# A new order of the same instructions: three tables of a planned kernel replaced

## The chip, the cores and the metric

The kernel runs on one core of a Trainium2 chip. The metric is device time in microseconds (us). The kernel before took 600.57 us in the median of 3 runs (599.95 to 601.61).

## The reference

An attention over local windows and block summaries, and then a layer norm with a two-layer network on its result:

```python
k_sum = k.reshape(B, H, nb, 32, D).max(axis=3)          # B, H, S, D = 4, 8, 768, 64
v_sum = v.reshape(B, H, nb, 32, D).mean(axis=3)
scores_l = where(|i - j| < 16, scale * q @ k.T, -1e9)
scores_s = scale * q @ k_sum.T + log(32)
a = softmax(concat([scores_l, scores_s]))
attn = a @ concat([v, v_sum])                            # -> x: (4, 768, 512)
xn = (x - mu) / sqrt(var + 1e-6) * g_ln
out = x + max(xn @ w_ch1, 0) @ w_ch2                     # w_ch1: 512 x 2048
```

## The kernel before, in words

The rows of x are cut into 24 blocks `T` of 128; attention goes in 48 half blocks `t` (four heads each), the network in 12 groups `g` of two blocks. Attention of batch 0 (`early_...`, t below 12) works in float32; the later ones split q, k and v into two float16 parts (`load_q`, `load_k`, `load_v`, `qk`, `softmax`, `transp`, `pv`). The weights are fetched in 32 pieces of 512 KB (`fetch_w`, m = 0 to 31), decoded (`dec_w`, three instructions on VectorE and a sum of squares on ScalarE), scaled by groups (`scale_w`) and converted to two float16 parts (`conv_w`). `g1` and `g2` are the first and second layer of groups 0 to 4; `sp1`, `sp2` and `sw2` do the same for the later groups with fewer products (Strassen-like, with operands made by `combine` and `combine2`). `batch(b)` reads K, q and V of the next batch (`batch_k`, `batch_q`, `batch_v`: a DMA into one of two staging buffers, a reduction on VectorE, absolute values on ScalarE), and `batch_s` makes the scales of the float16 parts.

Nothing is issued as it is written. Each function above is a step; steps are collected first (797 of them) and then recorded in the order of the table `ORDER` (`record_steps`, L230). Recording gives each operation (3501 in all) its dependences and decides who holds a shared buffer or PSUM bank after whom; the bank of each PSUM tile comes from the table `BANKS` (L578). Then `issue` (L538) lays the operations out on the five engines with a list of costs: an engine takes, among what is ready, the operation with the lowest number in the table `RANKS`. The numbers are a permutation of 0 to 3500. All DMAs are issued by SyncE (SP), in its order. In gaps of TensorE that the plan foresees early on, short transposes are put in as filling (`spare`).

A staging buffer is named by `stage_in` (L674): in batch 1 the pieces go in turn into `qs` and `bst` by the parity of a number, so `batch_q(1,5)` and `batch_v(1,3)` share `bst`, and `batch_v(1,2)` and `batch_v(1,4)` share `qs`. The DMA of the next piece waits until ScalarE has taken the absolute values of the one before.

Steps named in the prediction: `batch_k` (L685), `batch_v0` (L735), `batch_v` (L752), `batch_mask` (L793), `early_pv` (L966), `ln` (L1028), `fetch_w` (L1069), `dec_w` (L1078), `scale_w` (L1098), `conv_w` (L1129). In the trace every instruction has the line L563, from which `issue` calls it, so tiles tell them apart: `in` are the staging buffers (`in_ks`, `in_vs`, `in_qa` in DRAM), `raw` and `wf` belong to `dec_w`, `wp` to `conv_w`, `wps` and `wsc` to `scale_w`, `pp` and `pT` are the transposes of batch 0, `vst` and `tail` the sums of V, `a` and `h` the products of the network.

Of the kernel before, what the change touches and what calls it, by code (L numbers as in the profile page):

```python
# [22 lines left out]
B, H, S, D = 4, 8, 768, 64  # L23
DM, DFF = 512, 2048
P = 128
# [35 lines left out]
    "%d%r%e%s%v%w%x&%%y%z%{&$&'%|&)%}&#&+$Y&D&&&(&*&.&/&>&X&`&]&W&f&C&V&Y&Z&[&a&^&k&b&c&d&e&g&_&h&l&m&n&o&p&r&u&v&t"
    "&w&x&y&{'>&?'=&z&@&B&R&H&J&N&P&L&F&G&I&T&q&s'<'?'G'@'A'C'E'F'H'I'R&|&K&M'Q'P'S'u'T'U'B'D'V'$'%'Y'J'L&O&Q&S&U'Z"
    "'[']'w'^'_'v'x(8'W'X'{'y'z'|&}&i&j'#':'6','-'8'0'.(6'2(7(9(#(,()(-(2(%($('(((+(&(0(*(A(3'K'M'N'O'`'a(:'b(<'/'1"
    "'3(J'}(G(C(;(=(>(P'4'5'7'9';(B(D(L(E(F(H'c(K(M(N(O(Q'&'''(')'*(I(R(S'd'i'k's'o'g'm'q'e'f'h'j'l(/(1(?(@'n'p'r't"
    "'+(T(Z(.(4(5(_(V(^(U(](`(a(b(d(g(h(W(l(q(f(i(s(j(z(k(m(r(t({).(c(e(w(u(v(x(y)4(|(})#)$(n(o)%)&)')=)()/)7)0)1)9"
# [17 lines left out]
    "%m%W%o%V%U&A&J&V&i&t'C'G'H'?%'%b%l%t%}$o%B%K%Q%[%e%k%s%y&%&-(H&D'@&`'3&3&}&:'D%H&>&y'9'J'U'`'o'x&S&^&b&d&k%+&$"
    "&<&B&M&Y&a&j&n'R&/'r&,&2&I&O&W&]&e&v&|'='K'V'Q'Y'W%.'>'O'X'n%S%^$|%(%p(4(<(B(G&5&f&u&{&F&X&c&l&s&w'#&Z&_&p&x'$"
    "',')'/'N'S'^'c'a'[&T&U&Q&P&R&h'%'('.'0'4':'|&q(0&o&r'+'1'2'<'E'P'B'T'_'e'k'l'm'h's'y'}(&(,'5'8&z'&'-'g'p(%(K'7"
    "'I'u(_'Z(=(J(Z'z(5(@(T'F(#(-(I(R(P(W(O(N(U(S(`(e)C)Y)`*'*N*S*Y*Z*W*[(?(3(C(9(7()(E(L(:(p(t(y(|)#(}({)<'w(((/(;"
    "'j'q't'v'{(*(.(6(1(8(>).)4)?)F(M(Y(b(z(u)')G)^(F(h)/)3''(X(s)+)8'L'f($(+(V([(^(a('(f(o(r(x)%)2)7)B)Q)5)9)$)-)("
    ")0)s)h)J):(w)&),)=)K)W)R)E)x)[)}+2)c*^);'M(](d)I)P*:)n*A***G*Q*2*V(c(m(l(i(j(n)L)e)X)i)N)O)V)S*a*f(Q(g(q)@)d)f"
    "(v)A)H)k*/*4)1)T)Z)_)b*8*K*P)*)6)j)p)t)w*&*)*.*1*5*7,3*;*>*=*B*C*H*?*D*e*l*y+)*M*X*g*}*s+,+6+])a)g)l)o)D)r)v)z"
    ")|)>*%*6*`*r)M)m)q)U)y*#*+*0){*$*(*,*@*J*O*R*T*],<*_*d*b*h*j*o*n*q+8+=+F+x+C+X+b,&*z+'+-+o)u*<*F*U*x+$+#)]*3*9"  # L90
    "*k*v*E+/+4+9+;*L*{+&+++1*c*p+K+P,%,+,0,8,.,5*i*m+7+:+>+A+5+D+E+L+N+T+[+I+Y+Q+^+g+k+},),@,L,W,V,X,T+G+J+S+W+V+Z"
    "+m+c,7,Q,],y+i+u,#,Z+a+|,$,',*,-,4,F,;,N,S,2,A,J,Y,h-(-3-0-/-4-8->-C-H-U-X*t+d+j+v+z*w+O+U+_+e,(,,,1,6,=,?,C,H"
    ",_,d,K,R,O,U,l,q,^,k,f,o-&-2-<,a-5-)-=-D.,-s-@-V-F-P.4.F.M-x.*.1+l(A,P,j+%+*+3+0-E,|-S-[-k-u.$-d-q-{*I*u*|+(+<"
    "+?+.+@+H+B+f+n+p+q+s+r+t,/,9,>,B,D,G,E,`,e,r-#,w(D)),p-*%N%g-+-?'*']'b-7-;,:,[,u--*-+`+h,m-%,z+M+R,i,t-N-Y-]-a"
    "-i-o-v-r-z(k+y-L-`.#.&.+.7.=,{-$-_-e-6-O-W-h.'./.;.3.B.5.:.@.C.I.L.N.i.o.}/*/7/</A/N/V/]-9-c-g.2-f-}.8.D.U.].j"
    ".e.p.b.`.h.g.s.y/#/+//-p.6.<.n.9.W.a.r-G-K.0.X/,/4/C/:/H/G/8/J/B/P/S/X/b/g.|/9/>/O,I,g,n,s,x,}.J.q.v/@-,-1-./U"
    "/j-:-J-T-b-l-t.Y.c.m.{/F/W/c/x.l.t/%/0.P/&/-/R/`/h/p/}/1/5/[/m.?.H.Q.w0d/|0j02/M/t0&04-B-A-M/(/30-0@0E0L-j-m.["
    ".f/o/E/i0#0N0%0,000;0(0:0>0C0O0V0^0n0s._.d/2/K/$/=/D0=0{1-121B1=0G0h111<0M0]0c0g0l090u1&0P0`/Z/y0*16.k.x/w071Y"
    "0<0A1_1q1d1t1m1x1j1h1p1o/;/?/60H0T2-25292D0a0_0Z232;,c-Z-y.%.(.>.-.A.E.S.G.^/)/./I/_/L/f/e/v/Q/T141D18151E1?1L"
    "1R1]1f1n190D1C0Y1J1(1Q1Z1^131K1T0U0w1:1c1;1V1a1w211g2'2J2O2:2H2B2M2]2V2`2Y1@1e1i2L2f2Q2i3/381|2$2)2/242b2o3-35"  # L100
    "2A2C2G2n322q3(2|3,2x3$2}3*31393>3K3Q0m0t0y0|1'1+/a/k/u0'0+060?0F0J171A1F303:3G3N1b1k1u1}2=2I2P2g3%4=3C3M3U3Z2("
    "262K2_2R2Z2d3@1M1P2>2S1s1y2*2.2&2?2E2{3o+{+w,M,v%X,b-I-Q-n-'-R-^-|.)-w.K.R...O.T.V.u.z.Z/Y/^/'/q/{0)0/0.05/d03"
    "0$0K080b0f0z1%0S0p0v1)1,1*1.0}1H1N1U1r1v2#2s3)1/1W1[/n/s/r0W0k2N2e2k2u3=3F3P3T3W3Y3`3i3n1$0o0r2U2m2h2l2r3#3+3x"
    "4)4%403b3l3q3v2t2z2w3k3r3S4G4(4t414<4z5%2W2[3t4&494A4F4M3I3B3?4B4K3'3E3y4,4$464*4;4>4E4N4^4l575F5M5R3}3w3{5A5G"
    "2j2v3;3J3[4O3g4Y3s4e3|4C4J4n5+592T2p2y4.4T444X4]4k4_4g4f4m4d4a4j4h4p4v4|5)5.3z454?4@4D4I3L3a4#4i5#5'555*5<505("
    "535-5D5H5L5X5a/l/z010B0I0Q0R0X0[0e0i0q0x1#101>1G1O1I1S1X1l1z2,2227282@2<3H2F3R3V3]3c3f3h3m3p423u474H4R4Z4o4b4q"
    "4r4y5g5k5l5n656B6F6H6K6N6Q6R6W6q4L4U4c5J5U5b5e5q5{646;5&5,585@6S6^6h6m5;5C5Q5]6&6.686>6{7'7/765_5i5r5y6o696u6A"
# [1532 lines left out]
```

## Time and profile before

| | |
|---|---|
| median of 3 runs | 600.57 us |
| the profiled execution | 602.07 us, its span 599.9 us |
| mean granted clock of TensorE | 0.997 |
| TensorE busy | 586.2 us, 98% |
| VectorE busy | 525.1 us, 88% |
| ScalarE busy | 424.4 us, 71% |
| GpSimd busy | 193.9 us, 32% |
| moved by DMA | 96.07 MB, mean 160 GB/s |

PE is TensorE, PEld its weight load, DVE VectorE, ACT ScalarE, POOL GpSimd, SP SyncE. Matmuls are pipelined, so records of neighbours overlap. An idle time in brackets stands before the instruction and names what ended it. Durations and starts are us from the start of the span, if not marked ns.

### The profile page before, as it was taken

The page shows a single profiled execution, that of the slowest core. Times are in us where ns is not written, and L with a number is a line of the kernel's source. Part 1 is how long each engine was busy: PE and PEld are TensorE (multiplying, and loading weights), DVE is VectorE, ACT ScalarE, POOL GpSimd, SP SyncE. Part 2 cuts the span into 40 slices and gives each one's busy share as a digit, 9 for nine tenths or more (in the row PEclk, how much of TensorE's full clock was granted, in tenths as well). Part 3 has the DMA queues.
Part 4 walks back from the last instruction along what each step waited for, and adds up shares of the span by engine and source line. Part 5 has one row for each costly group of instructions (what it writes and reads, how often), then busy time and mean ns, then how long its engine had stood idle before and what let it go on. Part 6 is the DMA issues. An engine that isn't in the chain of part 4 may idle for free.

```text
span 599.9 us, 16301 instructions
## 1 busy us (share of the span) xinstructions
PE 586.2 (98%) x6048; PEld 444.9 (74%) x6048; DVE 525.1 (88%) x1351; ACT 424.4 (71%) x968; POOL 193.9 (32%) x355
## 2 busy tenths in 40 slices
...
GB/s 311 313 310 209 97 296 101 237 54 170 245 203 180 210 180 196 178 146 190 211 197 205 167 195 121 116 196 173 113 94 180 89 151 54 92 65 46 80 1 36
DMA packets 138175, 96.07 MB, mean 160 GB/s; under 512 B 96112, under 2 KB 120944, under 8 KB 138096
## 3 DMA queue, kind: packets, MB, share of 16 engines
...
HBM read 66.27 MB, written 6.29 MB: 121 GB/s over the span
## 4 chain that ended last, share of the span: by engine, by line
PE 68%; DVE 14%; ACT 8%; DMA 6%; issue 3%; POOL 1%; SPq 1%; ACTq 0%; DVEq 0%; POOLq 0%
PE a L563 26%; PE qx L563 11%; PE h L563 9%; PE qz L563 6%; PE o L563 4%; PE s L563 4%; PE a_x L563 3%; DVE wf L563 3%; PE qy L563 2%; PE a_y L563 2%; DMA raw<-in_w 2%; DMA in<-in_vs 2%; ACT p L563 1%; DVE raw L563 1%; DMA in<-in_ks 1%
## 5 line engine op out<-in xcount | busy, mean ns | idle before, releaser
L563 PE MATMUL a<-wp,hh 128*128 128x512 f16 x640 | 190.4, 379 | 0.0
L563 PEld LDWEIGHTS <-wp 128*128 128x128 f16 x1968 | 152.1, 98 | 17.5 <-DVE wp L563 0.8
L563 PE MATMUL a<-wp,hl 128*128 128x512 f16 x320 | 121.3, 379 | 0.0
L563 PEld LDWEIGHTS <-hh 128*128 128x128 f16 x736 | 69.1, 98 | 60.2
L563 PE MATMUL h<-xs,wp 128*128 128x256 f16 x960 | 110.0, 273 | 0.6 <-DVE wp L563 0.6
L563 POOL TENSOR_TENSOR p<-p,p 128x512 f16<-128x512 f32 x72 | 76.7, 1074 | 72.8 <-ACT p L563 40.0
L563 ACT ACTIVATE p<-p,mn 128x184 f32<-128x184 f32 (+1 forms) x192 | 76.6, 441 | 13.4 <-DVE mn L563 13.1
L563 PEld LDWEIGHTS <-wd 128*128 128x128 f16 x1176 | 70.5, 98 | 5.1 <-issue 0.3
L563 PEld LDWEIGHTS <-hl 128*128 128x128 f16 x368 | 36.0, 98 | 38.3
L563 DVE CUSTOM_DVE_ANT_0 p<-s,mask,sv 128x184 f32<-128x184 f32 x144 | 53.0, 399 | 3.4 <-PE s L563 1.8
L563 ACT ACTIVATE in<-in 96x512 f32<-96x512 f32 (+2 forms) x66 | 39.1, 594 | 15.5 <-DVE vsum L563 7.3
L563 PE MATMUL qx<-xs,wp 128*128 128x128 f16 x672 | 42.6, 219 | 0.0
L563 POOL COPY ksg<-ksum 128x48 f32<-128x48 f32 x48 | 17.4, 363 | 64.5 <-DMA ksg<-in_kt 56.5
L563 ACT CAST p<-p 128x512 f16<-128x512 f32 x72 | 34.2, 507 | 0.6
L563 DVE SCALAR_TENSOR_TENSOR x<-a,wsc,x 128x512 f32<-128x512 f32 x40 | 29.6, 743 | 4.7 <-PE a L563 4.6
L563 ACT ACTIVATE qhl<-qs,sv 128x512 f16<-128x512 f32 x36 | 25.7, 717 | 9.2 <-PE s L563 7.8
L563 POOL TENSOR_SCALAR rs<-mv 128x1 f32<-128x1 f32 x24 | 9.9, 414 | 67.9 <-DVE mv L563 67.0
L563 DVE SCALAR_TENSOR_TENSOR qhl<-qs,sv,qhl 64x512 f16<-64x512 f32 x36 | 28.0, 779 | 2.1 <-ACT qhl L563 2.1
L563 ACT ACTIVATE hh<-h 128x512 f16<-128x512 f32 x40 | 23.7, 597 | 7.5 <-PE h L563 7.4
L563 ACT ACTIVATE v<-vst,sv 128x512 f16<-128x512 f32 x36 | 26.0, 723 | 3.9 <-PE o L563 3.9
L563 DVE SCALAR_TENSOR_TENSOR v<-vst,sv,v 128x512 f16<-128x512 f32 x36 | 28.4, 790 | 0.2 <-ACT v L563 0.2
L563 PE MATMUL o<-v,pT 128*128 128x65 f16 (+1 forms) x720 | 27.5, 193 | 0.0
...
## 6 DMA issues: line engine op xcount, KB each, us to landing
...
```

Of the source, the lines that this page charges most:

```text
L563: getattr(getattr(nc, self.ops[i].engine), op)(*a, **k)
```

## The change

The tables `ORDER`, `BANKS` and `RANKS` are replaced; no other line changes. 716 of 797 steps stand at another place in `ORDER`, 9 places off in the mean and 120 at most; 180 of 314 PSUM tiles change the bank. The tables come from a search by replays in which each operation's duration deviates at random; this search is not in the kernel. The first lines of each:

```diff
 ORDER = (
-    "#)$Z#+$i$g#'#7#%#5#6#3$h#,#k#8$k$[$l#(#W#4###l#/#1#2$^$_$v#D#*#=#>#?#@#A#B#C$f#$$]$m#&#9#;#:#E#F#G#H#K#I#X#J#L"
...
+    "#)#7#+#,#'$g#%#3#k#5#6$Z#4#(#W#8$k$i$[$l#D#/#1#2$h$b$f$^#$$_$v$]#*#=#>#?#@#A#B#C##$m#&#9#;#:#E#F#G#H#X#K#I#J#L"
...
 BANKS = (
-    "61751223542751020346542121677316033561042161105264013266573725130751461516457422130647301102513756424013747051"
...
+    "77341333542751020346527101647231033461042160175264013625773254307561462215164574031647301102513756421405437014"
...
 RANKS = (
-    "#B#;#8#>#3&4&8#&$F#1#/#.#4#0#H#I#X#E#5#%#'#(#-#+#*#K#T#M#a#]#9#S#Y#=#W#V$:$=#j%0#f#k#G$1$/$3$7$<#:#y#|$)$5#,$e"
...
+    "#=#9#;$J#.#g#3&'#'#J###E#1#I#7#4#)#2#$#-#(#/#,#*#0#8#:#?#>#@#D#B#F#G#H#}#&$5$:#A$-#%$w$|#C$($0$4$9$<&%#<#x#|$+"
...
```

Sorted by their ranks, the operations of one engine come in the order in which that table wants them there. In the kernel before, this order is that of the trace, at each of VectorE's 1159 and ScalarE's 869 operations. So the tables can be read as orders. Decoded, the stretches that the prediction speaks of (`#n` is the n-th operation of a step, counted from 0):

```text
SP, from 13 us (DMAs):
  before  w7  v0(3) v0(4) v0(5)  w5  v0(6)  batch_k(1,0)  tail0 tail0 tail1 w6
  after   w7  v0(2) v0(3) v0(4) v0(5)  tail0  batch_k(1,0)  v0(6)  w5  tail0 w6
VectorE, from 23 us:
  before  dec_w7#2  conv_w3  batch_k(1,0) kmax  conv_w0  dec_w5#0  conv_w1
  after   dec_w7#2  batch_k(1,0) kmax  conv_w0  conv_w1  conv_w3  dec_w5#0
ScalarE, from 28 us (c: the six copies of batch_v0(6)):
  before  c c  exp  c  exp  c  pT  c  pT  c  dec_w5
  after   c c c c c c  conv_w2  pT  pT  exp
staging buffer bst of batch 1, who holds it after whom:
  before  k(1,1)  q(1,5)  v(1,3)  v(1,5)  v(1,1)  v(1,7)
  after   k(1,1)  v(1,3)  q(1,5)  v(1,5)  v(1,1)  v(1,7)
SP, from 72 us:
  before  v(1,2) q(1,5) w20 w18 w19 w22 w30 v(1,3) w21 v(1,4) w23 w31 v(1,5)
  after   v(1,3) w20 v(1,2) w18 w19 w30 w21 w31 w22 w23 v(1,4) q(1,5) v(1,5)
VectorE, from 81 us (sums of v(1,n), d: dec_w):
  before  d18#0 conv_w15 d18#1 hl d18#2 d20#0 v(1,3) p d20#1 d19#0 d20#2 v(1,4) d19#1 d21#0 d19#2
  after   v(1,2) hl d18#0 v(1,3) d18#1 d20#0 d18#2 d20#1 d19#0 d20#2 d19#1 d21#0 d19#2 d21#1 p d21#2 v(1,4)
TensorE, from 88 us:
  before  g2(8) g2(2) g2(3) scale_w(1,2) early_pv(8,1) g2(10) g2(11) g2(9) scale_w(1,3) g2(10) g2(11)
          g1(12) early_transp(9,1) early_transp(9,0)
  after   g2(10) g2(2) early_pv(8,0) early_pv(8,1) g2(3) scale_w(1,2) g2(11) g2(8) g2(9) g2(10) scale_w(1,3)
          early_transp(9,0) g2(11) early_pv(9,0) g1(12) early_transp(9,1)
GpSimd, from 133 us:
  before  go_late load_k(12,0) combine(0,0) go_late  ln(4)#2-4  batch_mask(1)  ln(5)#2,#3 load_k(13,1) ln(5)#4
  after   load_k(12,0) go_late go_late combine(0,0) batch_mask(1)  ln(4)#2-4  combine(0,0) load_k load_k  ln(5)#2-4
```

## Rows read from the trace of the kernel before

**Rows 1.** The page: busy time, share and instructions of each engine.
```profile
PE 586.2 (98%) x6048; PEld 444.9 (74%) x6048; DVE 525.1 (88%) x1351; ACT 424.4 (71%) x968; POOL 193.9 (32%) x355
```

**Rows 2.** Stretches: length, busy us (instructions) of PE, PEld, DVE, ACT, POOL; clock, DMA, GB/s.
```profile
15.00:30.00 15.00, 12.59 (x63) 6.81 (x62) 13.53 (x46) 12.64 (x35) 2.48 (x7) 1.00 1.06 313
...
45.00:60.00 15.00, 15.00 (x134) 13.31 (x133) 15.00 (x47) 15.00 (x51) 2.17 (x8) 1.00 0.63 209
...
90.00:105.00 15.00, 13.30 (x77) 7.12 (x75) 14.93 (x35) 9.71 (x23) 1.43 (x2) 1.00 0.32 102
...
165.00:180.00 15.00, 15.00 (x170) 13.42 (x168) 15.00 (x37) 12.12 (x28) 8.61 (x11) 1.00 0.99 204
```

**Rows 3.** TensorE's waits, 45 to 600 us: total, times, longest.
```profile
PE pp L563 <- ACT x L563: 1.0, 1, 1.0
PE wps L563 <- ACT wf L563: 1.0, 1, 1.0
PE h L563 <- DVE wp L563: 0.6, 1, 0.6
PE s L563 <- ACT pT L563: 0.2, 1, 0.2
PE qx L563 <- ACT two L563: 0.2, 1, 0.2
```

**Rows 4.** The chain that ended last: start, us, what.
```profile
18.76 8.09 DMA in<-in_ks
...
78.82 9.22 DMA in<-in_vs
...
457.51 4.30 DMA a<-x_a
...
480.27 1.50 PE qx L563 x24
```

**Rows 5.** Timeline of VectorE and ScalarE near 27 us.
```profile
26.88 0.55 DVE L563 TENSOR_REDUCE kmax<-in 128x12 f32<-128x384 f32 x1 [1.47 <-DMA in<-in_ks]
...
27.46 0.53 ACT L563 ACTIVATE in<-in 128x384 f32<-128x384 f32 x1 [1.21 <-DVE kmax L563]
```

**Rows 6.** Two stretches by engine, as rows 2.
```profile
28.00:36.00 8.00, 5.83 (x49) 4.79 (x47) 7.00 (x23) 7.78 (x20) 0.53 (x3) 1.00 0.90 328
38.00:41.00 3.00, 3.00 (x16) 2.56 (x17) 2.70 (x13) 2.67 (x7) 1.27 (x5) 0.50 1.09 214
```

**Rows 7.** Timeline of TensorE, 26 to 38 us.
```profile
28.90 0.49 PE L563 MATMUL o<-vst,pT 128*128 128x130 f32 x2 [0.73 <-ACT vst L563]
...
36.27 0.49 PE L563 MATMUL o<-vst,pT 128*128 128x130 f32 x2 [1.01 <-ACT pT L563]
```

**Rows 8.** Timeline of SP's queue near 17 us.
```profile
17.41 0.83 SPq L563 DMA_DIRECT2D raw<-in_w  x1
```

**Rows 9.** Timeline of VectorE, 80 to 96 us.
```profile
88.06 0.68 DVE L563 TENSOR_REDUCE vsum<-in 96x16 f32<-96x512 f32 x1 [2.54 <-DMA in<-in_vs]
```

**Rows 10.** Timeline of SP's queue, 64 to 84 us.
```profile
72.73 0.33 SPq L563 DMA_DIRECT2D in<-in_qa  x1
74.18 4.55 SPq L563 DMA_DIRECT2D raw<-in_w  x5
78.82 0.69 SPq L563 DMA_DIRECT2D in<-in_vs  x1
```

**Rows 11.** Timeline of ScalarE near 78 us.
```profile
77.77 0.61 ACT L563 ACTIVATE in<-in 128x512 f32<-128x512 f32 x1
```

**Rows 12.** Timeline of TensorE near 93 us.
```profile
93.63 0.39 PE L563 MATMUL wps<-wacc,ones 128*128 128x4 f32 x2 [0.95 <-ACT wf L563]
```

**Rows 13.** GpSimd and VectorE near 141 us, and GpSimd's group over the span.
```profile
141.22 3.18 POOL L563 TENSOR_SCALAR rs<-mv 128x1 f32<-128x1 f32 x1 [2.96 <-DVE mv L563]
...
142.95 1.40 DVE L563 SCALAR_TENSOR_TENSOR wp<-raw,wsc,wp 128x512 f16<-128x512 f32 x2
...
L563 POOL TENSOR_SCALAR rs<-mv 128x1 f32<-128x1 f32 x24 | 9.9, 414 | 67.9 <-DVE mv L563 67.0
```

More of the change, by code (lines that the diff above doesn't have):

```diff
@@ L61 @@
[L61 to L65, printed above, removed]
@@ new lines @@
+    "#<#M#N#O#Q#R#P#S#T$$#a#Y#Z#[#_#]#^#`#m#l&,&2&3&1&4#b#c#d#g#u#e#f#h$7$n$o$p$r$s$`$w$a$x$y$z${$|$}%##-#n#o#q#r#p"
+    "$%$q$j%/$c%($e%*#U#V$d%)#s#t%+#.$&$'$)$*$($8$+$,#v#w#y#x#{#z#|$H#i#0%-%,$-$.$/$1$@$0$3$2$4$5#j$u$t%'%&%$%K$9$:"
+    "$<$;$>#}$#$6%@%B%?%A%.%0%5%6%7%3%8%1%2%D%C%4%F%H%J%E%G%I&0&-%:%N%=%Z$=$?%9%M$A$Q&6&8&:&9$B$C$F$D$E$G&?%;&5%<%Y"
+    "%%%L%O%P%R%S%Q%W%h%X&<%V$I%>%[%]%^%_%`%a%k%j%l%e%f%t$J$K$M$L$O$N$P&;%i%g%u%T%n%U%o%c%q%m$R$S$T$W$U&7&=&D&E$V$X"
+    "%b%p$Y%d%r&A%s%v%w%x&%%y%z%{%}&#%|&'&)&$&&&(&*&+&.&/&>&X&]&`&C&V&W&Y&Z&[&^&_&a&k&b&c&d&m&e&g&l&n&f&h'<&t&u&v&w"
@@ new lines @@
+    "&x&y&{&o&p&r&@&B&H&R&J&T&N&P&L&F&G&I&K&M'=&q&s'B'>'?'@'A'C'P'F'E&z'G'H'I'J&|'K'Y'Q&}'R'S'T'U'Z'u'[']'w'v'x(8'L"
+    "(7'^&O&Q&S&U'$'D'V'W'X'y'z'|&i&j'#':'0'6','-'2(6(9(C'.'/'1'3(A'M'N'O'`'_'a'b(<'c(:'8'{'}(G'%(;(=(>(P(J'4'5'7'9"
+    "';'&''(B(D(L(E(F(H(I(K(M(N(O(Q(R(S'd'i'k'o'g'q's'm'e'f'h'j'l'n'p'r't'(')'*'+(?(@(T(Z(#(,()(-(2((('(%($(+(&(0(3"
+    "(.(1(/(4(V(W(*(5(_(](^(`(l(g(f(h(U(a(b(i(j(k(m(s(r(c(d(e(w(n)%(o(p(q(t(u(v(x(y({(|)4(z(})#)$)&)')=)())).)/)7)0"
+    ")1)2)3)5)9)6)H)8):);)B)C)K(X(Y([)<)>)?)Q)D)E)F)G)I)J)a)M)Z)L)N)])O)[)^)_)`)y)b)@)A)x)w)z)P)R){)S)})|*#*))*)+)d"
@@ L83 @@
[L83 to L107, printed above, removed]
@@ new lines @@
+    "$1$Y$=&9#k#v&-#z%@#[#K#P#Q#S#V#U#Y#]#N#^#_#c$K$X$b$k#R#O$W$c$p$x%%%+%0%6%A%:%7%?%<#+$8$;$E$H#6#`#L#W#a#h#X#Z#b"
+    "#i#q#l#w#s#t#{#y$##p#r#m#o#n$'$.$2$6%;%B%]%a%d#d#M#T#e#f#j#u$>$?$@$C$F%G%M$3$%$7$,$B%J%U%k%n%z%h%o$*$)$$$/$&$I"
+    "$O$U$h$`$i%$$r%K%R%e%2%W%j%s&)&4&<$N$V$Q$P$S%/%F#5$D%)%3%8&e'6%=&&':'n't(<&2'I$M$[$l$d%m$q$o$z$v%`%y$^$]$Z$_$f"
+    "%x&$&0&:&G&J&O&B&E$A$G$L$T$a$g$j$m$s$y$t%(%-%D%L%*%5$R%9%>%E%P$e%C%I%S%^$u${%'%.%f%p%u%{&(&3'w'^'f&?'0&;'8&u'A"
+    "$n%H%Y%_%i%t&+&F&T%g%b%w%q%O%Z%V%Q%[$}%1%&%r&|'<'c%#%l%v&#&.%4'H'P'k'v&*&5&8&=&C&M&g&o%|'p(%(;(?&A&I&Y&v&{'('4"
@@ new lines @@
+    "'9'%&@&i&x'>%,%}&7&>&Q&U&a&n&w&H&K&L&_&6&/'b&1&,&f&k&}'E'J'W'S'['X&D&S&^&X&j&m'#&Z&b&c&s&z'*'&'.'F'K'Q'V'R'N'7"
+    "'3&V&]&`&d&l%c(*(4(=(B(E(J(N(R&[&R&W&N&P&h'$'5'1';'@'D()&q(-&t&p'''+'-'/'='C'M'T'`'e'h'j'l'g's'{'}($((&r&y','Y"
+    "'d'q'|'2'B'z(]'m(>(I(U'y(7(D(Q'?(f(r)$)H(&(.(L(H(O)6)K(W(T(Z(V(h(q'Z'o'r'u'x(,(6(C(2(9(A(M(S(^(b(n)()1)8(z)/)D"
+    ")V(F([(e(v'L'U'a(#(Y(_(a(d'i(g(t)#(|)+)=)E)A)I)3)<)%)));)B)')0)*)4*1)c):)@)7)>*7)g*>)k*I*T***9)F)M)p)U*#+7)[*Y"
+    "'O('(+(G(K(@(i(s(x(u({(w)9)f)i)m)o)J){*%*(*-)v)z*E*W*^*_*Z*`)5)Y)^)b)e(c(j(m(o(p(k(P)&).)2)R)X)])t)}(y)Z)_)L)q"
```

108 lines of the change are left out of this document (59 added, 49 removed).

## The prediction

> **What bounds the kernel now.** I read the engine table first: TensorE is busy for 586.2 of 599.9 us, VectorE for 525.1 [rows 1]. A busy TensorE may still be one whose matmuls come slowly, so the second view is the table by stage. From 165 us to 585 every stretch of 15 us has TensorE at its full 15.00 (one has 14.84), as in the row of 165 to 180; what it lacks is in front, 12.59 of 15 from 15 to 30 us and 13.30 from 90 to 105 [rows 2]. The third view says whom it waited for after 45 us: five waits, together 1.0 + 1.0 + 0.6 + 0.2 + 0.2 = 3.0 us [rows 3]. So no order of the same instructions can win more than 3.0 us behind 45 us, plus what is lost ahead of it.
>
> What sets those waits is not TensorE. The chain of work that ended last runs, in its first 120 us, over transfers, ScalarE and VectorE: a load of K (`in_ks`) that takes 8.09 us to land, and one of V sums (`in_vs`) that takes 9.22 [rows 4]. From 162 us on it is nearly all TensorE, with one detour from 441 to 480 us over VectorE, a transposing DMA of 4.30 us and ScalarE, back to the matmul at 480.27 [rows 4].
>
> **The change part by part.** No operation is added or removed. The three tables give a new order on every engine and new PSUM banks; so each step's cost is a wait that goes, comes or moves. I decoded the rank tables (the lists stand in the section on the change) and looked up each of the five waits, and those ahead of them, in the new order.
>
> Step 1, the load of K at 18.76 us. VectorE sat 1.47 us before the `kmax` at 26.88, and ScalarE then 1.21 us before the absolute values at 27.46 [rows 5]. ScalarE has hardly another gap between 28 and 36 us (7.78 of 8.00 busy [rows 6]), and the copies behind it feed TensorE: it waited 0.73 us for `vst` at 28.90 and 1.01 for `pT` at 36.27 [rows 7]. Before, the 512 KB of weight block 5 were issued at 17.41 [rows 8], ahead of the load at 18.76 [rows 4]; now they come behind it. At the 313 GB/s of that stretch [rows 2] 512 KB are 1.7 us, so the load lands at about 25.2 in place of 26.85, `kmax` ends at 25.7, and ScalarE, which ends its work before it at 27.46 - 1.21 = 26.25, no longer waits. That is -1.2 us on ScalarE's chain. The six copies of `batch_v0(6)` also stand together now, without two exponentials and two other copies between them. The lower bound is the 0.7 + 0.7 + 1.0 us that TensorE waited for ScalarE in this stretch (-2.4; the second `vst` wait is about as long as the first), the upper is a loss: the new order puts `kmax` ahead of three VectorE conversions, not one, so if the load lands no earlier, VectorE stands from about 24.7 to 26.9, 2.2 us in place of 1.5, with all three behind it: +0.7. I take -1.2, the wait on the engine that is full.
>
> Step 2, the load of V sums at 78.82 us. VectorE waited 2.54 us for it at 88.06, its longest wait [rows 9]. Why was it late? It uses a staging buffer that held a piece of q before it: that piece was issued at 72.73, its absolute values were taken at 77.77, and only then could SP issue the load, at 78.82, behind five weight blocks issued from 74.18 [rows 10, 11]. In the new order the two have changed places in the buffer: `batch_v(1,3)` follows `batch_k(1,1)` directly and should go out where the q piece did, near 72.7, ahead of all eight weight blocks. Even with 9.22 us it would land by 82, and VectorE wants it at about 83.9. The wait goes. The last decoding that `scale_w(1,2)` needs, `dec_w(19)`, also has 0.9 us less VectorE work ahead of it (the summed durations of what stands in front, old order against new). TensorE's wait for it, the one with 0.95 us at 93.63 [rows 12] (1.0 in the list of waits), therefore has 2.5 + 0.9 us of earlier supply against it, and on TensorE one more `early_pv` in front: -1.0. Bounds: -1.0 (all of it) and 0, if another load takes the place of this one. The candidate is `batch_v(1,4)`, now behind all eight weight blocks: issued near 82.9 and landing 9.22 us later at 92.1, against a VectorE that wants it at about 90.7. That would be a wait of 1.4 us, but behind `dec_w(19)`, so not ahead of this matmul.
>
> Step 3, the two waits that follow: 0.6 us for converted weights, 1.0 for ScalarE's `x` before a group of transposes [rows 3]. The conversions keep their place on VectorE within 0.8 us of work, and VectorE is 2.5 us earlier, less 1.4 if the wait above comes; on TensorE a transpose and an `early_pv` now stand in front of `g1(12)`. The 0.6 goes. Of the 1.0 I count 0.4, because ScalarE's copies of `x` still follow two sums that VectorE has to deliver. Together -1.0; bounds -1.6 and 0.
>
> Step 4, all the rest. Behind 108 us TensorE waited 0.4 us in 490 [rows 3]; this can hardly get better and can get worse. The bounds are 0 and the 4.30 us of the transposing DMA in the detour [rows 4]; I take +0.4, as much again as is there, the nearest row.
>
> Step 5, the clock. From 38 to 41 us the granted clock is 0.50, the level of 1.2 GHz, after a stretch from 28 to 36 in which TensorE had 5.83 of 8.00 us of work [rows 6]. At 2.4 GHz these 3.0 us would be 1.5. With step 1 TensorE idles less just ahead of it, so it may go; with new gaps it may come twice. Bounds -1.5 and +1.5; I take 0, as no row shows which.
>
> Step 6, between 139 and 148 us, at no cost as TensorE has no wait there [rows 3]. GpSimd's `rs` of layer norm 5 took 3.18 us at 141.22, against 414 ns in the mean of 24 [rows 13]. The new order puts the mask of batch 1 ahead of layer norm 4's chain on the same engine, and seven conversions and loads nearly in a row on VectorE ahead of it. The Trainium skill (SBUF — State Buffer, Who interferes with whom) states that a VectorE instruction with two inputs in SBUF blocks a GpSimd instruction that reads SBUF for its whole length. The trace agrees: the 3.18 us ended at 144.40, and the last two of VectorE's run of such instructions at 144.35 [rows 13]. By that rule GpSimd would stand again, for one such 3.18 us, which speaks against this part of the new order; without the rule it would stand not at all. Either way the sum is the same while TensorE has other matmuls to do, and up to 3 us more if it has not; 0.03 of the slower case is for that.
>
> The sum: -1.2 - 1.0 - 1.0 + 0.4 + 0 = -2.8 us. The profiled execution took 602.07 us (span 599.9 and 2.2 around it), so the changed one would take 599.3. It lies 1.5 us above the median of the runs shown, 600.57, so on that footing I predict 600.57 - 2.8 = 597.8 us.
>
> **The rivals.** First, the gain of the start is given back (same). VectorE is fully busy from 45 to 60 us [rows 2]; if TensorE comes 1.2 us earlier and VectorE does not, the time returns as a wait in between, and of steps 2 and 3 only one wait goes: -1.0 + 0.4, so 600.0 us. For it: VectorE has as little air as TensorE there. Against it: VectorE too was held by the same load, for 1.47 us.
>
> Second, the detour from 441 to 480 us becomes a wait (slower). There TensorE's next product hangs on VectorE, a transposing DMA and ScalarE, and it was in time by nothing: TensorE already waited 0.2 us at its end [rows 3]. Many steps move most in this later part (batch 2's loads by some 68 places of 797, `split1(12)` by 40). If the new order puts one more transfer like the 4.30 us one into that chain, TensorE waits 4.3 us, and with half of my gain 600.57 - 1.4 + 4.3 = 603.5 us. It decides from the point where the added wait exceeds the 2.8 + 1.8 us that separate forecast and a measurable loss. Against it: that chain begins at a TensorE product itself, so it moves with TensorE, and on TensorE the old and the new order differ by two places in the mean.
>
> Third, the low clock comes a second time: +1.5 us on the first rival, 601.5, the same within what can be told. That the order on the chip is not the decoded one speaks against itself: on VectorE and ScalarE the old table gives the trace's order at every operation.
>
> **How the numbers follow.** A change of 0.3% or 1.8 us is about what a measurement here can tell from none. Forecast, 595 to 598.7: 0.56. Given back, with or without the clock, 598.8 to 602.4: 0.28. The detour or another new wait: 0.16. So faster 0.56, same 0.28, slower 0.16. The lower end is the sum with the bounds of steps 1 and 3 and half the clock: -2.4 - 1.0 - 1.6 + 0 - 0.7, 594.9. The upper end leaves out two thirds of the slower case: 602.6. The forecast's own range is 594.9 to 598.7.
>
> **What would show it.** Step 1: no wait of VectorE or ScalarE on `in_ks` near 25 us, and ScalarE's copies over a microsecond earlier. Step 2: `in_vs` issued near 73 us, the 2.5 us wait of VectorE gone, and no wait of `wps` on ScalarE. Step 3: the row of 90 to 105 us with TensorE at 14.5 or more. Step 4: TensorE at 15.00 in every row from 165 to 585. Step 5: one stretch at 0.50, no longer than 3.4 us. I am wrong if the five waits are gone and the span is not shorter, which would mean new waits ahead of 45 us, or if TensorE waits over 1 us anywhere behind 165.

## The result, and the profile after

The changed kernel took 603.77 us (median of 5 runs, 603.12 to 604.51) against 600.57 for the kernel before (599.51 to 601.61): a ratio of 1.0053, 95% interval 1.0036 to 1.0070. It is slower by about 3.2 us. Forecast were 597.8 us and a range of 594.9 to 602.6. The profiled execution after is its median one, 603.77 us (span 602.0, clock 1.000); that of before lay 1.5 us above its median, so the two spans differ by less than the two kernels do. The prediction says that no operation is removed. That holds for the 3501 operations, but not for the filling transposes that the plan puts into foreseen gaps of TensorE: they fell from 20 to 13, all between 10 and 16 us, and so TensorE's instructions from 6048 [rows 1] to 6041.

The page and the stretches of the kernel after (columns as [rows 1, 2]):

```profile
PE 585.1 (97%) x6041; PEld 442.7 (74%) x6041; DVE 522.3 (87%) x1351; ACT 424.2 (70%) x968; POOL 189.6 (31%) x355
```

```profile
15.00:30.00 15.00, 13.19 (x70) 7.42 (x68) 14.87 (x47) 13.80 (x37) 2.05 (x8) 1.00 1.10 340
90.00:105.00 15.00, 13.60 (x96) 8.98 (x94) 15.00 (x34) 12.35 (x30) 1.47 (x2) 1.00 0.51 158
165.00:180.00 15.00, 14.81 (x139) 12.05 (x139) 14.73 (x41) 11.12 (x28) 5.58 (x11) 1.00 0.80 199
345.00:360.00 15.00, 13.86 (x231) 12.37 (x229) 11.63 (x28) 12.20 (x27) 4.09 (x9) 1.00 0.80 189
390.00:405.00 15.00, 13.51 (x162) 9.84 (x160) 11.38 (x30) 8.64 (x18) 2.14 (x7) 1.00 0.81 171
...
28.00:36.00 8.00, 7.23 (x65) 6.24 (x63) 7.52 (x29) 7.94 (x23) 2.15 (x4) 1.00 1.04 354
38.00:41.00 3.00, 3.00 (x28) 2.48 (x27) 2.97 (x17) 3.00 (x9) 0.58 (x4) 1.00 0.90 288
```

The front is better in every row: all three engines do more from 15 to 30 us [rows 2], TensorE fills 7.23 of 8 us from 28 to 36 and the clock stays up behind it [rows 6]. But from 345 us on TensorE lacks 1.14 and 1.49 us in two stretches in which it had been full (the rows of before):

```profile
345.00:360.00 15.00, 15.00 (x249) 13.66 (x248) 13.05 (x36) 13.26 (x28) 4.93 (x8) 1.00 0.86 196
390.00:405.00 15.00, 15.00 (x178) 11.12 (x177) 13.00 (x34) 10.95 (x23) 4.61 (x9) 1.00 0.68 197
```

TensorE's waits after 45 us say the same. Of the five of [rows 3] only the one for ScalarE's `x` is left, shortened to 0.2 us, and eight new ones have come, 7.4 us together in place of 3.0; below them the two of over 1 us behind 345 us, with their starts (one of 0.58 lies between, at 372.88):

```profile
PE qy L563 <- DVE hl L563: 1.5, 1, 1.5
PE pp L563 <- DVE hl L563: 1.4, 1, 1.4
PE o L563 <- ACT pT L563: 1.2, 1, 1.2
PE a L563 <- DVE hl L563: 1.1, 1, 1.1
PE h L563 <- DMA xs<-x: 0.9, 1, 0.9
PE a L563 <- DVE x L563: 0.6, 1, 0.6
...
PE pp L563 <- ACT x L563: 0.2, 1, 0.2
```

```profile
357.65 0.60 PE L563 MATMUL a<-wp,hh 128*128 128x512 f16 x2 [1.14 <-DVE hl L563]
...
402.55 0.62 PE L563 MATMUL qy<-xs,wp 128*128 128x128 f16 x8 [1.49 <-DVE hl L563]
```

To see where the lead goes I made a ledger. Each matmul of the trace gets the median distance from its start to the next one's, over its kind and shape (216 ns for 128x512 in float16); without the filling transposes they sum to 571.4 us of work. The time at which a given amount of work is done, less that work, is what TensorE has lost up to there (us, one profiled execution each):

```
work done       15     30     45     90    150    300    330    405    570
before       12.87  18.84  19.47  22.76  23.98  24.42  24.46  24.63  25.02
after        11.69  14.74  15.38  17.74  21.60  22.25  22.37  26.69  27.11
early_new_92 13.13  16.11  16.74  18.35  19.55  20.50  20.96  21.86  22.45
```

After is 4.1 us ahead at work 30, 5.0 at 90, 2.4 at 150, 2.1 at 330; then it loses 4.3 us in 75 and ends 2.1 behind. (In the trace after, work 330 is done at 352 us and work 405 at 432.) Two places are to be explained: 95 to 155 us and 350 to 405 us. The losses below are from the same ledger, one profiled execution each, and such an execution has its own scatter. Of all twenty traces, the five kernels with the old front have lost 18.3 to 20.5 us at work 45 (median 19.0), the fifteen with the new front 15.1 to 16.9 (median 16.4). So of the lead of 4.1 us that this pair shows there some 2.6 are the order's; the rest is these two executions. Between work 90 and 150 the seven other kernels with the unedited new order up to 300 us lose 2.0 to 5.5 us, where this trace of after loses 3.9.

### The profile page after: what moved, and what is told of

It reads as the page before. It is cut to its first block, busy times and chain, and to the rows that moved or that the text cites. A ratio compares the mean times of both kernels' runs of the same rounds, so it can differ in the third digit from the quotient of the medians.

```text
span 602.0 us, 16272 instructions
## 1 busy us (share of the span) xinstructions
PE 585.1 (97%) x6041; PEld 442.7 (74%) x6041; DVE 522.3 (87%) x1351; ACT 424.2 (70%) x968; POOL 189.6 (31%) x355
## 4 chain that ended last, share of the span: by engine, by line
PE 64%; DVE 17%; DMA 9%; ACT 5%; issue 3%; POOL 2%; SPq 0%; ACTq 0%; DVEq 0%; POOLq 0%
PE a L563 24%; PE qx L563 11%; PE h L563 7%; PE qz L563 6%; PE o L563 4%; PE a_x L563 3%; PE s L563 3%; DVE wf L563 3%; PE a_y L563 3%; PE qy L563 3%; DVE p L563 2%; DVE wp L563 2%; DMA in<-in_ks 2%; DVE raw L563 2%; DVE hl L563 2%
## 5 line engine op out<-in xcount | busy, mean ns | idle before, releaser
L563 ACT ACTIVATE p<-p,mn 128x184 f32<-128x184 f32 (+1 forms) x192 | 78.1, 445 | 16.9 <-DVE mn L563 16.4
L563 ACT ACTIVATE in<-in 128x384 f32<-128x384 f32 (+2 forms) x66 | 39.7, 602 | 13.5 <-DMA in<-in_qa 3.2
L563 POOL COPY ksg<-ksum 128x48 f32<-128x48 f32 x48 | 18.3, 384 | 59.6 <-DMA ksg<-in_kt 43.7
L563 DVE SCALAR_TENSOR_TENSOR hl<-h,hh 128x512 f16<-128x512 f32 x40 | 27.0, 679 | 6.9 <-ACT hh L563 6.9
L563 PEld LDWEIGHTS <-pT 128*128 128x128 f16 x720 | 25.7, 98 | 2.9
```

What stands on the lines that cost most here:

```text
L563: getattr(getattr(nc, self.ops[i].engine), op)(*a, **k)
```

## The experiments

All were timed in five rounds beside the kernel before; a ratio is to that, with its 95% interval. All leave the computation as it is. The tables are decoded, changed and encoded again, so an edit is given as the order of an engine's queue, with the step, the number of its operation and its tiles (`sp16,0#22` is operation 22 of `sp1(6,0)`). In these kernels `issue` puts the operations out by their ranks alone and takes the fillings from a list (13 with the new front, 20 with the old), so their rows name L561; with the unchanged tables of either kernel this gives every engine the same instructions in the same order.

**The two orders put together.** An operation belongs to the front if the new plan starts it before a given time; the front comes from one kernel, the rest from the other.

```diff
-RANKS, ORDER, BANKS: all new
+early_new_64, _92, _123, _146: new in front of 64, 92, 123, 146 us, old behind
+late_new_146: old in front of 146 us, new behind
```

> New tables up to 64 us only. This has step 1 of the prediction (the load of K ahead of weight block 5) and the whole new start with its clock, but not step 2 (the load of V sums near 73 us). TensorE leads by 4.0 us at that point. Theory A: 596.5 us, and the old waits at 88 us on VectorE (2.5 us) and at 93.6 us on TensorE (1.0 us) are back. If the lead of 4 us meets a VectorE that is not ahead, waits of 1 to 3 us between 64 and 120 us and 598 to 600 us.

> New tables up to 92 us (where both plans have started the same operations), old ones behind. TensorE leads there by 5.0 us. Theory A: the old order of the rest keeps it, 595.6 us, with its own waits near 102 and 106 us. Theory B: the lead is gone by 180 us, 600 us.

> New tables for everything that the new plan starts before 146 us, old tables for the rest. By the traces TensorE stands 3.6 us ahead of the old kernel at that point, and the new order loses 5.7 us behind it. Theory A (the loss belongs to the new order of the later part itself): the lead stays, 600.6 - 3.5 = 597.1 us, and TensorE waits behind 165 us as little as before, under 1 us. Theory B (the loss is the lead given back: VectorE, ScalarE and the DMAs of the later part cannot go faster, whatever the order, so a TensorE that comes earlier waits for them): waits of 2 us or more behind 165 us with the old order too, and 600 to 602 us.

> The other way round: old tables for what the old plan starts before 146 us, new tables for the rest. Theory A: the late loss is there without any lead, 600.6 + 5.7 to 6.7 = 606.3 to 607.3 us, with the waits of 1.1 to 1.5 us between 352 and 402 us. Theory B: without the lead there is less to give back, 602 to 603 us, and the waits between 352 and 402 us shrink to under 1.5 us in sum.

> The new order for what the plan starts before 123 us, the old behind it: between early_new_92 (598.83) and early_new_146 (605.59). Theory A (the 3.9 us wait of early_new_146 at 156 us was made by the seam of the two orders, and the lead is lost by single waits): this one takes on the changed kernel's waits at 97.7 and 101.5 us, 1.15 and 0.25, perhaps the one at 119 (1.37), in place of one of 1.0, and has no wait over 1 us between 125 and 330 us: 599.2 to 600.4. Theory B (a lead of TensorE is lost wherever the old order goes on behind it): 602 us or more, with a wait of over 2 us between 125 and 165 us.

| | us | ratio |
|---|---|---|
| early_new_64 | 599.48 | 0.9975 (0.9962 to 0.9987) |
| early_new_92 | 598.83 | 0.9959 (0.9944 to 0.9974) |
| early_new_123 | 601.98 | 1.0016 (0.9999 to 1.0033) |
| early_new_146 | 605.59 | 1.0075 (1.0059 to 1.0090) |
| late_new_146 | 606.36 | 1.0088 (1.0067 to 1.0110) |

The new order is worth 0.4% up to 92 us, 2.5 us, and loses it between 92 and 123. Behind 146 it loses with no lead at all in front of it: the ledger of late_new_146 goes from 26.0 at work 330 to 30.7 at 405, 4.7 us where after loses 4.3, as its Theory A had it. With the old order behind, early_new_64, _92 and _123 lose 0.9 to 1.2 us there, early_new_146 2.3. So most of the late loss belongs to the new order there; it is not a lead handed back. The parts do not add up: -2.5 us up to 92, +3.4 from 92 to 123 and +5.3 behind 146 make +6.2, and the changed kernel stands at +3.2, so waits at the seams, where the two orders meet, are among them. early_new_92 beats both kernels, but lies between its two theories (595.6 and 600). early_new_146 says little: most of its loss is one wait of 3.87 us at 160 us, at the seam, where VectorE stands 1.60 us for an `in_vs` in front of the softmax operations whose end TensorE waits for, and from 159.4 us on, as the wait ends, the granted clock is 0.50 for 3.4 us. early_new_123 missed Theory A's 599.2 to 600.4: its waits at 99.6 and 121.2 us are 1.89 and 1.49, longer than those of after, so part of its loss may be the seam's.

**Step 1 undone in the best front.**

```diff
 # SP in early_new_92
 fetch_v05#0
+fetch_w5#0
+fetch_v06#0
 fetch_tail0#1
 batch_k1,0#1   in<-in_ks
-fetch_v06#0
-fetch_w5#0
```

> early_new_92 (new order up to 92 us, old behind it; 598.83 us) with one part undone: the load of weight block 5 and the last load of batch 0's V sums go ahead of the first load of K again. Theory A (step 1 is what the front gains, 1.2 us): VectorE waits for in_ks again, about 1.5 us, ScalarE behind it, and the time is 0.9 to 1.5 us longer than early_new_92, 599.7 to 600.3. Theory B (the gain ahead of 45 us comes from the rest of the new order there, the copies standing together and the low clock that is gone): within 0.5 us of early_new_92, 598.4 to 599.3. If the low clock comes back with the wait, 600.5 to 601.5.

599.14 us, ratio 0.9969 (0.9955 to 0.9983): 0.10% or 0.6 us above early_new_92, with intervals that overlap. The wait did come back, as the timeline of VectorE and ScalarE shows (start and duration in us, engine, operation, tiles; in brackets the idle time before and what ended it):

```profile
26.00 0.55 DVE L561 TENSOR_REDUCE kmax<-in 128x12 f32<-128x384 f32 x1 [1.23 <-DMA in<-in_ks]
26.59 0.52 ACT L561 ACTIVATE in<-in 128x384 f32<-128x384 f32 x1 [0.28 <-DVE kmax L561]
```

1.23 us on VectorE and 0.28 on ScalarE, near 26 us, cost nothing that these runs can tell. The times alone do not shut out Theory A (0.9 to 1.5 us); the ledger speaks for Theory B, as at work 90 the trace of w5_first has lost within 0.1 us what that of early_new_92 has.

**Single waits mended.** Each edit lets the operation that TensorE waits for pass others in its queue.

```diff
 # repair_three: ScalarE at 355 us (likewise x<-a at 372, hh and hl<-qz at 401)
+sp16,0#22    hh<-qz
 load_k35,0#2 kh<-keys
 load_k34,1#2 kh<-ksg
-sp16,0#22    hh<-qz
 # repair_six also: pT<-pp at 97, hl<-h at 118, the DMA xs<-x at 148
 # early_92_sums: early_new_92 with rc and x<-o,rc ahead of scale_w's sum at 98
```

> The changed kernel with five operations put elsewhere in the queues of ScalarE and VectorE, for its three waits of TensorE between 352 and 405 us (1.14, 0.58 and 1.49 us): the conversion hh<-qz goes ahead of a kh<-keys that waits for GpSimd; x<-a goes ahead of a kl and an hl; hh<-qz and hl<-qz go ahead of a qhl<-qs and an hl<-seven. Theory A (the loss behind 300 us is these queues putting an operation that TensorE needs next behind one that still waits): all three waits go or fall below 0.3 us, 2.6 to 3.2 us off the changed kernel, 600.6 to 601.2 us in its own terms. Theory B (the loss behind 300 us comes from the stretch as a whole being fuller, or from the PSUM banks; a wait removed in one place comes back at the next): the waits turn up within 20 us at other matmuls, under 1 us gained, 602.8 to 603.8 us.

> As repair_three, and three more waits of the changed kernel by the same means: the copy pT<-pp ahead of two conversions wp<-raw (wait of 1.15 us at 97.7 us), hl<-h ahead of four operations of VectorE (1.37 us at 119.2 us), and the transposing DMA xs<-x ahead of three loads of vst and a store (0.86 us at 152.4 us). Theory A: the lead of 5.0 us that the changed kernel has at 92 us is kept to the end but for some 0.8 us of small waits, 6.0 to 6.6 us off the changed kernel: 597.2 to 597.8 us, faster than the kernel before. Theory B: each repair moves the wait on, no more than 2 us off, 601.8 us or more.

> early_new_92 (598.83 us) with its largest wait taken out in the way of repair_three: the two operations rc and the four copies x<-o,rc of one half block go ahead of scale_w's sum, a sum of V and a g2 on VectorE and of an absolute value on ScalarE, so that the transposes pp at 101.4 us no longer wait 0.96 us for ScalarE's x. Theory A (a wait before a TensorE that has work behind it is worth its length): 597.8 to 598.2 us. Theory B (the wait turns up at a later matmul of the same stretch): 598.6 to 599.2 us.

repair_three 603.26 us, 1.0029 (1.0017 to 1.0041); repair_six 603.14, 1.0033 (1.0018 to 1.0049); early_92_sums 599.93, 0.9976 (0.9959 to 0.9993). In ratios repair_three is 0.24% or 1.4 us faster than the changed kernel, with intervals that overlap, for 3.2 us of mended waits. The waits of 1.14, 0.58 and 1.49 us fell to 0, 0.2 and 0.3 (by the ledger), but 1.4 us came at 414 (`qx` on ScalarE's `two`) and 0.6 at 381 (`qz` on a DMA), and the loss between work 330 and 405 is still 3.4 us. In repair_six the three early ones gave nothing more; in place of the wait of 1.37 us at 119 one of 1.83 came, on ScalarE's `p`:

```profile
98.07 0.49 PE L561 MATMUL o<-vst,pT 128*128 128x130 f32 x2 [0.25 <-ACT pT L561]
...
103.20 0.55 PE L561 MATMUL pp<-ident,p 128*128 128x128 f32 x3 [0.77 <-ACT x L561]
...
121.50 0.55 PE L561 MATMUL pp<-ident,p 128*128 128x128 f32 x3 [1.83 <-ACT p L561]
```

In early_92_sums 0.96 us at `pp` became 1.0 at the next `h`, on VectorE's `x`, and 0.8 us of `wps` came ahead of it. Theory B holds for the early waits and mostly for the late ones: I read them as places where a late chain shows, not as what makes it late.

**What is late in front of 350 to 405 us.** I compared the start of each operation in the two traces. Between 300 and 400 us two groups of steps move furthest: the last five staging pieces of batch 3 with the sum over their largest values (9 to 30 us later) and the eight small transfers `vst<-vsum` (`batch_vput(3,·)`, 3 to 12 us later), which went out singly or in twos and threes from 371.5 us on in the kernel before and now go out late, six in a row; no other operation outside TensorE moves by more than 10.5 us. SP's queue before:

```profile
371.54 0.82 SPq L563 DMA_DIRECT2D vst<-vsum  x1
...
377.21 1.26 SPq L563 DMA_TRANSPOSE room<-x_s  x1
...
382.46 2.30 SPq L563 DMA_DIRECT2D vst<-vsum  x3
```

SP's queue after, and ScalarE behind it:

```profile
379.72 1.56 SPq L563 DMA_TRANSPOSE room<-x_s  x1
381.34 0.83 SPq L563 DMA_DIRECT2D vst<-vsum  x1
...
385.13 0.80 SPq L563 DMA_DIRECT2D vst<-vsum  x1
...
387.51 4.95 SPq L563 DMA_DIRECT2D vst<-vsum  x6
392.56 0.45 SPq L563 DMA_DIRECT2D ksg<-in_kt  x1
```

```profile
391.01 0.72 ACT L563 ACTIVATE v<-vst,sv 128x512 f16<-128x512 f32 x1 [2.19 <-DMA vst<-vsum]
...
393.71 0.72 ACT L563 ACTIVATE v<-vst,sv 128x512 f16<-128x512 f32 x1 [1.03 <-DMA vst<-vsum]
...
397.65 0.60 ACT L563 ACTIVATE kh<-ksg,sv 128x368 f16<-128x368 f32 x1 [3.21 <-PE a L563]
```

ScalarE waits for the transfers themselves, and the `ksg` load queued behind the six comes so late that `kh` starts at 397.65 (GpSimd's copy into that `ksg`, 0.22 us, began at 397.39 after 10.08 us of waiting for the DMA and ended 0.04 us ahead of `kh`; the `a` that the row names is not among the tiles of `kh`). `kl`, `qz` and `hl` follow on VectorE, and `qy` waits 1.49 us at 402.55.

```diff
 # places in all queues, taken from the other kernel
+pieces3_old:      after, the five pieces old     pieces3_new:      before, the five pieces new
+pieces3_vput_old: after, pieces and vput old     pieces3_vput_new: before, pieces and vput new
+vput_old:         after, vput old                vput_new:         before, vput new
```

> The changed kernel with the last five staging pieces of batch 3 (K of head pair 3, q 4, 3 and 1, K of head pair 1) and the sum over its largest values put back to their old places in all queues; the new order has them 10 to 20 us later (the last kmax at 348.1 us in place of 328.5). Theory C (these late pieces fill the stretch of 330 to 405 us with loads and with work of VectorE and ScalarE, and that makes the waits there): the 4.3 us that TensorE loses between 330 and 405 us fall to 1.5 or less, 600.6 to 601.4 us in the changed kernel's own terms. Theory D (the loss there is the order of the rest, the pieces only came along): 603.0 to 604.3 us.

> As pieces3_old, and the eight small transfers that put batch 3's V sums behind the values (vst<-vsum), which the new order has 25 to 60 places later and six of them in a row at 387.5 us, back to their old places too. Theory C with both: the wait of 1.49 us at 402.6 us goes as well, as the loads behind the six transfers come earlier; 599.8 to 600.8 us. If only the first part matters: the same as pieces3_old within 0.5 us. Theory D: 603 us or more.

> The reverse: the kernel before with only these pieces of batch 3 and the eight transfers at the places that the new order gives them, all else old. Theory C: TensorE, which waits 0.2 us between 330 and 405 us in the kernel before, waits 2.5 to 4.5 there, 603.0 to 605.0 us. Theory D: within 1 us of the kernel before, 600.3 to 601.8.

> The kernel before with only the last five staging pieces of batch 3 at the places of the new order. Theory E: 0.5 to 1.0 us of waits between 330 and 360 us, none of over 0.5 us behind 380: 600.9 to 602.2 us. Theory F: 3 to 4.5 us of waits between 330 and 420: 603.5 to 605.3 us.

> The kernel before with only the eight transfers vst<-vsum of batch 3 at the places of the new order. Theory E (these transfers, issued in a row in front of the loads that ScalarE's v and kh wait for, make the waits from 385 us on): TensorE waits 2.5 to 3.6 us between 380 and 420 us and nothing between 330 and 360; 603.0 to 604.5 us. Theory F (the late pieces make all of it, by filling VectorE and ScalarE in front): within 1 us of the kernel before.

> The changed kernel with only the eight transfers vst<-vsum at their old places. Theory E: ScalarE's v no longer waits 2.19 and 1.03 us for them near 391 us, the load of ksg that kh waits for at 397.65 us is issued earlier, and the wait of 1.49 us at 402.6 us falls below 0.4; the waits at 357.7 and 372.9 us stay: 1.1 to 2.0 us off the changed kernel, 601.8 to 602.7. Theory F: 603.2 to 604.3 us.

| | us | ratio | lost, work 330 to 405 |
|---|---|---|---|
| pieces3_vput_new | 605.49 | 1.0065 (1.0042 to 1.0088) | 4.3 |
| vput_new | 603.69 | 1.0044 (1.0025 to 1.0063) | 2.9 |
| pieces3_new | 601.28 | 1.0016 (0.9996 to 1.0035) | 1.3 |
| vput_old | 606.99 | 1.0105 (1.0081 to 1.0128) | 6.6 |
| vput_old_two | 606.91 | 1.0103 (1.0079 to 1.0127) | 7.8 |
| pieces3_old | 609.31 | 1.0134 (1.0107 to 1.0161) | 3.8 |
| pieces3_vput_old | 612.26 | 1.0188 (1.0163 to 1.0213) | 7.4 |

vput_old_two is vput_old with the two edits at 355 and 372 us of repair_three; expected were 600.2 to 601.2 us, or 602.2 and more if a repair only moves the wait.

From the side of the kernel before the case is plain: both groups at their new places lose 4.3 us where it had lost 0.2. The eight transfers alone do most of it, and the waits of ScalarE are the ones foretold (vput_new, ScalarE, then TensorE):

```profile
389.17 0.72 ACT L561 ACTIVATE v<-vst,sv 128x512 f16<-128x512 f32 x1 [1.75 <-DMA vst<-vsum]
...
393.79 0.72 ACT L561 ACTIVATE v<-vst,sv 128x512 f16<-128x512 f32 x1 [2.21 <-DMA vst<-vsum]
```

```profile
400.82 0.83 PE L561 MATMUL qy<-xs,wp 128*128 128x128 f16 x12 [0.75 <-DVE x L561]
411.19 1.00 PE L561 MATMUL qx<-xs,wd 128*128 128x128 f16 x15 [1.72 <-ACT one L561]
```

That the changed kernel loses 4.3 us too is in part chance. Its wait at 402.55 us comes again at the same product in pieces3_vput_new (1.48 us at 404.59), but those at 357.65 and 372.88 have no counterpart there, and the 0.89 us at 414.13 has none in the changed kernel. So the two groups account for the wait at 402; what made those at 357 and 372 late is open.

From the other side all four forms became worse, against what I expected. pieces3_old and pieces3_vput_old have a seam: VectorE stands 3.99 and 3.91 us near 305 us for the `kmax` that was moved up, as the load for it was not ahead of it. vput_old has no seam. The wait at 402 us is gone, but a new one stands in front, and the clock falls with it (TensorE, two stretches, then SP):

```profile
385.73 0.84 PE L561 MATMUL qz<-room,wd 128*128 128x128 f16 x12 [3.40 <-DMA room<-x_s]
```

```profile
383.00:386.00 3.00, 0.27 (x5) 0.27 (x6) 0.42 (x1) 1.05 (x2) 0.00 (x0) 1.00 1.06 199
386.50:389.90 3.40, 3.40 (x29) 2.19 (x27) 1.88 (x8) 1.50 (x3) 0.70 (x1) 0.50 0.22 60
```

```profile
375.47 1.63 SPq L561 DMA_DIRECT2D vst<-vsum  x2
...
380.50 1.48 SPq L561 DMA_TRANSPOSE pT<-p  x1
382.08 1.59 SPq L561 DMA_TRANSPOSE room<-x_s  x1
```

So TensorE had 0.27 of 3 us of work, and 3.4 us at the level of 1.2 GHz followed, up to 1.7 us more (an estimate from the two levels) on top of the wait. SP waited 4.5 us there for one operation of VectorE, `v<-vst` of half block 34, and the transposing DMA is queued behind. VectorE in the kernel before, then in vput_old:

```profile
370.75 0.75 DVE L563 SCALAR_TENSOR_TENSOR v<-vst,sv,v 128x512 f16<-128x512 f32 x1
```

```profile
374.67 0.74 DVE L561 SCALAR_TENSOR_TENSOR v<-vst,sv,v 128x512 f16<-128x512 f32 x1
```

In vput_old it stands behind eight operations, six of which the old order has behind it. Two more runs put that operation back as well:

```diff
 # VectorE in vput_old_v34 (vput_old_v34_two: the edits at 355 and 372 us of repair_three too)
 sp26,0#4       x<-a
+load_v34#4     v<-vst
 softmax34,0#1 ... split215#5
-load_v34#4     v<-vst
```

> vput_old with one more operation moved: VectorE's v<-vst of half block 34, on whose end the transfers vst<-vsum wait, goes ahead of nine operations, to about 371.7 us in place of 374.7. Theory E (SP's queue stood for this operation): the transfers go out near 372.6 us, the wait of 3.5 us of qz<-room goes, and so does that of qy at 402 us, as in vput_old; left are 1.1 at 356 us and small ones: 1.5 to 2.2 us off the changed kernel, 601.6 to 602.4 us. Theory G (SP is too full in this stretch for the transfers to stand anywhere without harm): a wait of over 2 us stays between 375 and 395 us, 604.5 us or more.

> vput_old_v34 with hh<-qz ahead of the kh<-keys that waits for GpSimd and x<-a ahead of a kl and an hl. Theory E: of the 4.3 us that the changed kernel loses between 330 and 405 us no more than 1.2 are left, 600.4 to 601.4 us. Theory G: 604 us or more. If a mended wait comes back at the next matmul in line: 602 to 603 us.

602.50 us, 1.0031 (1.0016 to 1.0046), and 602.08 us, 1.0024 (1.0010 to 1.0039). Against vput_old, the move of one VectorE operation ahead of eight others is worth 0.7%, with the fall of the clock that goes with it. SP in vput_old_v34 (compare the rows above):

```profile
372.14 1.63 SPq L561 DMA_DIRECT2D vst<-vsum  x2
...
378.77 1.58 SPq L561 DMA_TRANSPOSE room<-x_s  x1
```

The loss between work 330 and 405 falls from 4.3 us to 1.9 and 1.5, and TensorE's wait for `room<-x_s` to 0.2 and 0.7. Theory G is out, and the waits went as Theory E had them. In units of the ratio the first run is 0.22% faster than the changed kernel (1.3 us of the expected 1.5 to 2.2), the second 0.29% (1.7 of the expected 2.4 to 3.4), both with intervals that overlap that of the changed kernel. Theory E in full (at most 1.2 us left) missed in the second: 1.5 us are left, and its time, 602.08, is that of the third reading, 602 to 603, in which a mended wait comes back. The changed kernel too has SP stand 4.2 us for this `v<-vst`, there at 375.84 us; the move of this operation alone was not run, so how the gain splits between it and the eight transfers is open. By the ledger most of what still parts the two from the kernel before is the loss between 92 and 155 us.

## Why the prediction was wrong

Step 4 failed. I took +0.4 us for "all the rest", as much again as the old trace showed of waits behind 108 us, with 4.30 as the bound. The changed kernel loses 4.3 us between work 330 and 405 alone, where the old one loses 0.2: the whole bound, in a stretch that I had counted as safe because TensorE was full in it. My own sign of being wrong, a wait of TensorE of over 1 us behind 165, came twice (1.14 and 1.49 us). What made the late loss, as far as the runs show it: staging pieces and eight small transfers that the new order issues later; at their new places in the kernel before they cost 0.65%, 3.9 us, the eight alone 0.44%, 2.6 us. The fault was in how I looked. I looked up in the new tables the waits that were there; a new order makes waits at places that had none.

**Step 1** (load of K, -1.2) happened: `kmax` ran at 24.60 with no wait. But that this wait was worth 1.2 us is not shown: with weight block 5 in front again the wait returns and no change of the time can be told. The new front up to 64 us as a whole is worth 0.25%, 1.5 us (0.8 to 2.3); that the forecast of 1.2 lies near it is luck as far as the load goes, and which part of the order there gives it is open.

**Step 2** (load of V sums, -1.0) was right in its waits (after):

```profile
69.41 0.33 SPq L563 DMA_DIRECT2D in<-in_vs  x1
...
72.84 0.33 SPq L563 DMA_DIRECT2D in<-in_vs  x1
73.28 5.05 SPq L563 DMA_DIRECT2D raw<-in_w  x7
```

```profile
88.47 0.68 DVE L563 TENSOR_REDUCE vsum<-in 96x16 f32<-96x512 f32 x1 [1.61 <-DMA in<-in_vs]
```

The load of `batch_v(1,3)` was issued at 69.41 us, earlier than the 72.7 that I had (that of 72.84 is `batch_v(1,2)`). The 2.54 us of [rows 9] (VectorE's longest wait ahead of 165 us, not of the whole span) and the wait of [rows 12] are gone, and the load that took its place made VectorE wait 1.61 us, where I had worked out 1.4. With the order of 64 to 92 us the ratio goes from 0.9975 to 0.9959, 1.0 us; the intervals overlap, so its worth is not shown.

**Step 3** (-1.0) failed too. The wait of 0.6 went and the one of 1.0 fell to 0.2, more than counted; but two new ones stand beside them (after):

```profile
97.71 0.49 PE L563 MATMUL o<-vst,pT 128*128 128x130 f32 x2 [1.15 <-ACT pT L563]
101.46 0.55 PE L563 MATMUL pp<-ident,p 128*128 128x128 f32 x3 [0.25 <-ACT x L563]
119.21 0.52 PE L563 MATMUL pp<-ident,p 128*128 128x128 f32 x3 [1.37 <-DVE hl L563]
```

TensorE comes sooner; VectorE, full there (14.93 of 15 us from 90 to 105 [rows 2], 15.00 after), does not. ScalarE is not full (9.71 [rows 2] and 12.35). From early_new_92 to early_new_123 the ratio rises by 0.57%, 3.4 us, and in the ledger after loses 3.9 us between work 90 and 150 where the kernel before loses 1.2. That is the first rival, priced too low; that VectorE's load is the reason is argued from these rows, not shown by a run.

**Step 5** (clock, 0): the stretch at 0.50 is gone in the profiled execution after, the favourable bound, but the new order did not remove it. Of the four other profiled kernels with the old front, three have the clock at 1.00 from 36 to 44 us (pieces3_new, vput_new, pieces3_vput_new), and late_new_146 has 0.50 elsewhere, for 6.8 us from 30 us on. It was a matter of the execution that was profiled, and 0 was the fair term.

**Step 6** (GpSimd's `rs`, 0): TensorE had no wait there, and the 3.18 us did not come back after, against what I had worked out; the group's mean fell from 414 ns [rows 13] to 240. The order decides it: in each of the ten kernels with the old order there the longest `rs` takes 3.18 or 3.19 us, in the ten with the new one 0.60 to 0.68. The longest in vput_new, then in the changed kernel with the VectorE instruction beside it:

```profile
139.66 3.19 POOL L561 TENSOR_SCALAR rs<-mv 128x1 f32<-128x1 f32 x1 [2.94 <-DVE mv L561]
```

```profile
135.59 0.60 POOL L563 TENSOR_SCALAR rs<-mv 128x1 f32<-128x1 f32 x1 [2.40 <-DVE mv L563]
```

```profile
135.42 0.71 DVE L563 SCALAR_TENSOR_TENSOR wp<-raw,wsc,wp 128x512 f16<-128x512 f32 x1
```

Here one VectorE instruction stands beside `rs` and not five (141.05 to 144.35 us before), and `rs` ends 0.06 us behind it, at 136.19. That agrees with the block that the Trainium skill (SBUF — State Buffer, Who interferes with whom) led me to allow for; what I had wrong is how many such instructions the new order puts beside `rs`.

The second rival had the sign and almost the size (603.5): a transfer in a chain that was in time by nothing. That its figure is near the measured 603.77 is luck: its place was wrong, 385 to 402 us and not 441 to 480, and so was its price's source: no transfer was slow; they were queued behind others. I gave it 0.16. What was left open is how the loss from 95 to 155 us splits among its waits: mending them one by one showed only that they move.
